# Attention and two gated layers: the maxima of k and q are bound behind the last VectorE operation of the iteration before

## The chip, the core and the metric

The program runs on one NeuronCore of a Trainium2 chip. The core has five engines with a queue of their own each: TensorE (PE in the profile, with PEld for its weight loads), VectorE (DVE), ScalarE (ACT), GpSimd (POOL) and SyncE (SP), which here only starts transfers between DRAM and the on-chip memory. Each queue is worked off in order; engines wait for one another through semaphores. The metric is the time of one execution on the device in microseconds (us), lower is better.

## What is computed

```python
# q, k, v: 8 batches, 8 heads, 576 tokens, 64 features, float32
q_s = exp(q - max(q, features)) ; q_s /= sum(q_s, features) + 1e-9
k_s = exp(k - max(k, tokens))   ; k_s /= sum(k_s, tokens) + 1e-9
attn = q_s @ (k_s^T @ v)                       # per batch and head
x = attn as 4608 tokens x 512 features
xn = x / sqrt(mean(x*x) + 1e-6) * rms_g
x = (silu(xn @ w_gate) * (xn @ w_val)) @ w_out # 512 -> 1536 -> 512
h = max(x @ w1, x @ w2, x @ w3)                # 512 -> 768
out = h @ w_out2                               # 768 -> 512
```

## The kernel before

The 4608 tokens are nine groups of 512: groups 0 to 7 are the first 512 tokens of one batch each, group 8 the last 64 tokens of all eight. Heads go in four pairs (128 features) per group. float32 products are made of three products of parts: an operand is split into a high part (`hh`, `xh`, `qh`, `kvh`) by ScalarE and the remainder (`hl`, `xl`, `ql`, `kvl`) by VectorE.

The first layer runs as 9 x 12 iterations: group g, block f of 128 of the 1536 hidden features. An iteration makes twelve gate products into the PSUM bank `pg` (L691), and twelve value products into `pv` (L703); ScalarE applies tanh (L697), VectorE multiplies it with the gate bank (L698), which empties that bank, then with the value bank (L709); ScalarE rounds the result to `hh` (L712), VectorE takes the remainder `hl` (L716). That is the last VectorE operation of the iteration proper. The output products of block f - 1 follow on PE (L720). There is one gate bank, so the next iteration's gate products need L698 done.

While group g goes through the first layer, the attention of group g + 1 (`nxt`) is prepared pair by pair: at f = 2p the maxima of k and q of pair p (L665, L666: `k_max` at L346, `q_exp` at L324); at f = 2p + 1 k's exponential and q's sum; at f = 2p + 2 q and k^T v are completed and the next pair is loaded; at f = 2p + 3 the attention product follows. For groups 2 to 8 (`by_feature`) q lies in memory twice, by token and by feature. The copy by token gives the statistics: VectorE's maximum (L326), POOL's subtraction (L336), ScalarE's exponential (L337), VectorE's sum (L304) and reciprocal (L307). Maximum and reciprocal are stored to a small DRAM array (L293) and read back spread over partitions (L299); with them POOL subtracts and multiplies on the copy by feature (L310, L315). Groups 0 and 1 (`COMPACT`) go another way. Beside this, group 0's iterations unpack the first layer's weights on VectorE and ScalarE, and groups 1 to 7 split the second layer's weights on ScalarE and POOL and store them to DRAM.

The code's order is not the queues' order. A scheduler places each engine's instructions when the program is built, by their dependencies and its own idea of durations; an instruction whose inputs and buffers it thinks ready may be placed long before the code around it. `k` and `q` tiles have two buffers, the transposed k for the maximum has one.

Of the kernel before, what the change touches and what calls it, by code (L numbers as in the profile page):

```python
# [8 lines left out]
F32 = mybir.dt.float32  # L9
# [38 lines left out]
def attention_moe_moe(ctx: ExitStack, tc: tile.TileContext, q, qt, k, kt, v, w1, rms_g, w2, w2_out, out):  # L48
# [14 lines left out]
    nc = tc.nc  # L63
# [52 lines left out]
    for i in range(2):  # L116
        t = one.tile([P, P], F32, tag=f"kv_raw{i}", name=f"kv_raw{i}")
# [168 lines left out]
    def load_by_feature(g, p):  # L286
        qT[g, p] = two.tile([P, N], F32, tag="qT", name=f"qT_{g}_{p}", bufs=1)
        nc.sync.dma_start(qT[g, p], qt[g - BY_FEATURE, p])

    def put_stat(g, p, i, stat):  # L290

        dst = stats_dram[NPAIR * g + p][i].rearrange("a (r t) -> r a t", t=4)
        nc.sync.dma_start(dst, stat.rearrange("r (a t) -> r a t", a=2))  # L293
# [30 lines left out]
    def q_exp(g, p):  # L324
        qm = two.tile([P, 24], F32, tag="qm", name=f"qm_{g}_{p}")[:, 0:8]
        nc.vector.tensor_reduce(qm, q_t[g, p], axis=AX.X, op=ALU.max)  # L326
        if g in COMPACT:
            qs = two.tile([P, 8], F32, tag="qs", name=f"qs_{g}_{p}")
            qsum[g, p] = qs
            nc.vector.tensor_scalar(qm, qm, -1.0, None, op0=ALU.mult)  # L330
            for i in range(8):
                head = q_t[g, p][:, i, :]
                nc.scalar.activation(head, head, AF.Exp, bias=qm[:, i : i + 1], accum_out=qs[:, i : i + 1])
            return
        put_stat(g, p, 0, qm)
        nc.gpsimd.tensor_sub(q_t[g, p], q_t[g, p], qm.unsqueeze(2).to_broadcast([P, 8, 64]))  # L336
        nc.scalar.activation(q_t[g, p], q_t[g, p], AF.Exp)  # L337
# [8 lines left out]
    def k_max(g, p):  # L346
        if g == NB:
            return
        km = two.tile([P, 1], F32, tag="km", name=f"km_{g}_{p}")
        nc.vector.tensor_reduce(km, kT_t[g, p], axis=AX.X, op=ALU.max)  # L350
        kmax[g, p] = km
# [11 lines left out]
    def make_kv(g, p):  # L363
        if g == NB:
            return
        pk = pair_bank(g, p, "pk", "a0")
        for c in range(5):
            nc.tensor.matmul(  # L368
                pk[:, 0 : P + 1], k_t[g, p][:, c, :], v_t[g, p][:, c, :], start=(c == 0), stop=(c == 4)
            )  # L370
        sm = two.tile([P, 1], F32, tag="ks", name=f"ks_{g}_{p}")
        nc.vector.tensor_scalar(sm, pk[:, P : P + 1], EPS_SM, None, op0=ALU.add)
        rs = two.tile([P, 1], F32, tag="kr", name=f"kr_{g}_{p}")
        nc.vector.reciprocal(rs, sm)
        raw = kv_raw[p % 2]
        for j in range(2):
            s = slice(64 * j, 64 * j + 64)
            nc.vector.tensor_scalar(raw[s, s], pk[s, s], rs[s, 0:1], None, op0=ALU.mult)
        if g not in WHOLE:
            kvh[g, p] = two.tile([P, P], F32R, tag="kvh", name=f"kvh_{g}_{p}")  # L380
            kvl[g, p] = two.tile([P, P], F32R, tag="kvl", name=f"kvl_{g}_{p}")
            split(kvh[g, p], kvl[g, p], raw)
        nc.sync.dma_start(kv_dram[p, :, g, :], raw)
# [122 lines left out]
    def normalise(g, p):  # L506
        if g == 0:
            nc.vector.tensor_mul(xraw[g, p], xraw[g, p], rstd[g][1])
            return
        nc.vector.scalar_tensor_tensor(  # L510
            xraw[g, p], xraw[g, p], gain[:, p : p + 1], rstd[g][1], op0=ALU.mult, op1=ALU.mult
        )
# [45 lines left out]
        for h in range(2):  # L558
            stage(0, h)

    acc, hh, hl = {}, {}, {}

    def out1(g, f):
        if f == 0:
# [82 lines left out]
    def iteration(g, nxt, f):  # L647
        ahead = g == 0 and f + 1 < NF1
        pair, odd = f // 2, f % 2

        if ahead:
            first.scale(f + 1, 0)
        if nxt is not None:
            by_feature = nxt >= BY_FEATURE
            if not odd and 1 <= pair <= 4:
                (q_by_feature if by_feature else transpose_q)(nxt, pair - 1)
                make_kv(nxt, pair - 1)
                if pair + 1 < 4:
                    load_pair(nxt, pair + 1)
            if not odd and pair < 4 and by_feature:  # L660
                load_by_feature(nxt, pair)
            if odd and 1 <= pair <= 4:
                make_x(nxt, pair - 1)
            if pair < 4 and not odd:
                k_max(nxt, pair)  # L665
                q_exp(nxt, pair)  # L666
            if pair < 4 and odd:
                k_exp(nxt, pair)
                (q_stats if by_feature else q_divide)(nxt, pair)
            if f == 10 and nxt in COMPACT:  # L670
                token_rstd(nxt)
            elif f == 10:
                variance(nxt)
                newton_step(nxt, 0)
                newton_step(nxt, 1)
            if f == 11:
                if nxt not in COMPACT:
                    newton_step(nxt, 2)
                for p in range(4):
                    normalise(nxt, p)  # L680
        elif f == 1:
            load_raw(0)
        if ahead:
            first.join(f + 1, 0)
            first.scale(f + 1, 1)
        wkey = (1, f)
        raw = g == 0 and f < NRAW
        xhs = [(rawh[p] if raw else xh[g, p]) for p in range(4)]
        xls = [(rawl[p] if raw else xl[g, p]) for p in range(4)]
        pg = bank("G", f"pg_{g}_{f}")  # L690
        product_in(pg, wh[wkey], wl[wkey], 0, xhs, xls)  # L691
        t = two.tile([P, N], F32, tag="t", name=f"t_{g}_{f}", bufs=1)
        if raw:
            u = two.tile([P, N], F32, tag="y", name=f"u_{g}_{f}", bufs=3)
            nc.vector.tensor_mul(u, pg, rstd[0][1])
            pg = u
        nc.scalar.activation(t, pg, AF.Tanh, scale=0.5)  # L697
        nc.vector.scalar_tensor_tensor(t, t, 1.0, pg, op0=ALU.add, op1=ALU.mult)  # L698
        if ahead:
            first.high(f + 1, 0)  # L700
            first.join(f + 1, 1)
        pv = bank("V", f"pv_{g}_{f}")
        product_in(pv, wh[wkey], wl[wkey], 1, xhs, xls)  # L703
        if nxt is not None and f == 11:
            for p in range(4):
                split_x(nxt, p)
        if raw:
            nc.vector.tensor_mul(t, t, rstd[0][1])
        nc.vector.tensor_mul(t, t, pv)  # L709
        hh[g, f] = two.tile([P, N], F32R, tag="hh", name=f"hh_{g}_{f}")  # L710
        hl[g, f] = two.tile([P, N], F32R, tag="hl", name=f"hl_{g}_{f}")
        nc.scalar.copy(hh[g, f], t)  # L712
        if ahead:
            first.low(f + 1, 0)
            first.high(f + 1, 1)
        nc.vector.tensor_sub(hl[g, f], t, hh[g, f].bitcast(F32))  # L716
        if nxt is not None and f == 9 and nxt not in COMPACT:
            split_squares(nxt)
        if f > 0:
            out1(g, f - 1)  # L720
        elif g > 0:
            out1(g - 1, NF1 - 1)
        if nxt in COMPACT and f == 10:
            spread_rstd(nxt)
        if g > 0 and nxt is not None:
            if g == 1 and f == 0:
                second.load()
                second.load()
            second.advance(f)
            if g == NG - 2 and f == NF1 - 1:  # L730
                assert not second.steps
        if nxt is None:
            if 1 <= f <= 3:
                fetch(2)
            if f in (4, 5):
                for n in range(4 * f - 16, 4 * f - 12):
                    combine(0, n)
            if f >= 6:
                for which in {6: (B11,), 7: (T2,), 8: (T1,), 9: (T3,), 10: (B21, B22), 11: (T4,)}[f]:
                    split_operand(which)  # L740
        if ahead:
            first.low(f + 1, 1)
            first.load(f + 4)
        if g == 0 and f == NRAW - 1:
            for p in range(4):
                normalise(0, p)
                split_x(0, p)

    for g in range(NG):
        nxt = g + 1 if g + 1 < NG else None  # L750
# [177 lines left out]
    for pr in range(NPAIR):  # L928
        behind = []
        for u in range(UNITS):  # L930
            fp, j = divmod(u, 3)
            if j == 0:
                t = {
                    key: two.tile([P, N], F32, tag=tag, name=f"t2_{pr}_{fp}_{tag}")
                    for key, tag in (((0, 0), "q"), ((0, 1), "k"), ((1, 0), "v"))
                }
# [22 lines left out]
    g = NG - 1  # L959
# [28 lines left out]
    for u in range(UNITS):  # L988
        fp, j = divmod(u, 3)
        pair = [bank(tag, f"p2_{g}_{u}_{tag}") for tag in (("G", "V"), ("a0", "a1"))[u % 2]]  # L990
        if j == 0:
            t = [two.tile([P, N], F32, tag=tag, name=f"t2_{g}_{fp}_{tag}") for tag in ("q", "k")]
# [82 lines left out]
```

## Time and profile before

| | |
|---|---|
| median of 3 runs | 1574.95 us (1574.34 to 1579.06) |
| profiled execution | 1573.16 us |
| its span, first to last instruction | 1571.4 us |
| busy share of the span: TensorE, VectorE, ScalarE, GpSimd | 97%, 60%, 37%, 17% |
| groups 1 and 2, from the first gate product of one group to the next | 127.4 and 123.9 us |
| groups 3 to 6 | 106.3 or 106.4 us each |

The profile is of one execution. Times within it count from the first instruction. A matmul's shown duration overlaps the next one's, so a busy TensorE need not be at its peak. Names are those of the program without buffer numbers; L698 is line 698.

### The profile page before, as it was taken

What the parts mean: (1) busy time and instruction counts of PE and PEld (TensorE: products, weight loads), DVE (VectorE), ACT (ScalarE), POOL (GpSimd) and SP (SyncE); (2) the same over time, 40 slices, a digit from 0 to 9 for tenths busy, and PEclk for the clock granted to TensorE, in tenths of its full rate; (3) what the DMA queues carried; (4) which work ended last, traced back from release to release, by engine and by line L of the source; (5) the groups of instructions that cost most, each with busy time, mean ns of one, the idle gap of its engine ahead of it and who ended that gap; (6) DMA issues with size and microseconds to landing.
All of it is one profiled execution on the core that took longest, in us unless ns stands there. A gap on an engine that the chain in (4) does not pass through costs nothing.

```text
span 1571.4 us, 19245 instructions
## 1 busy us (share of the span) xinstructions
PE 1517.6 (97%) x6790; PEld 1244.1 (79%) x6790; DVE 938.2 (60%) x1622; ACT 579.0 (37%) x1107; POOL 263.7 (17%) x307
## 2 busy tenths in 40 slices
PE   6899988889999999999999999999999999999999
PEld 4677876767888888888888888888888888888887
DVE  6999765754655546555444252527947937937722
ACT  6764434433433433334333231322412412413311
POOL 0000234233131131231321100001111111111100
PEclk8899999999999999999999999999999999999999
DMA  7842655564343442552433204026576486485573
GB/s 272 321 154 76 197 134 148 129 122 131 117 143 93 156 154 63 173 166 75 144 118 121 74 7 168 1 87 242 173 273 239 158 295 234 159 306 198 164 271 107
DMA packets 126065, 250.03 MB, mean 159 GB/s; under 512 B 26640, under 2 KB 51216, under 8 KB 125968
## 3 DMA queue, kind: packets, MB, share of 16 engines
q1 hardware_dynamic: 119056, 236.21, 46.3%
q10 hardware_dynamic: 6912, 12.59, 2.4%
q8 instruction: 54, 0.88, 0.2%
q14 instruction: 43, 0.35, 0.1%
HBM read 205.52 MB, written 43.22 MB: 158 GB/s over the span
## 4 chain that ended last, share of the span: by engine, by line
PE 75%; DVE 1%; POOL 0%; DMA 0%; issue 0%; ACT 0%; SPq 0%; ACTq 0%; DVEq 0%
PE pg L523 5%; PE acc L530 5%; PE acc L531 5%; PE acc L529 4%; PE pg L525 4%; PE pg L524 4%; PE pv L525 4%; PE pv L524 4%; PE pv L523 4%; PE p_a L530 4%; PE p_a L531 4%; PE p_a L529 4%; PE p_G L529 2%; PE p_G L530 2%; PE p_G L531 2%; PE p_V L531 1%
## 5 line engine op out<-in xcount | busy, mean ns | idle before, releaser
L698 DVE SCALAR_TENSOR_TENSOR t<-t,pg 128x512 f32<-128x512 f32 x106 | 72.6, 685 | 117.0 <-ACT t L697 115.4
L800 POOL TENSOR_TENSOR temps_wl<-temps_wh 128x512 f32<-128x512 f32 x36 | 48.3, 1341 | 438.3 <-ACT temps_wh L799 363.7
L712 ACT CAST hh<-t 128x512 fp32r<-128x512 f32 x108 | 66.8, 619 | 126.4 <-DVE t L709 125.9
L709 DVE TENSOR_TENSOR t<-t,pv 128x512 f32<-128x512 f32 x108 | 73.9, 684 | 65.2 <-PE pv L525 63.2
L716 DVE TENSOR_TENSOR hl<-t,hh 128x512 fp32r<-128x512 f32 x108 | 76.0, 704 | 52.6 <-ACT hh L712 52.3
L697 ACT ACTIVATE t<-pg 128x512 f32<-128x512 f32 x106 | 62.9, 593 | 87.9 <-PE pg L525 87.7
L529 PE MATMUL p_a<-x_wh,chunk 128*128 128x512 f32 x240 | 93.4, 389 | 0.0
L531 PE MATMUL p_a<-x_wh,chunk 128*128 128x512 f32 x240 | 93.4, 389 | 0.0
L530 PE MATMUL p_a<-x_wl,chunk 128*128 128x512 f32 x236 | 91.8, 389 | 0.0
L236 POOL TENSOR_TENSOR wq<-st,wq 128x256 fp32r<-128x256 f32 x84 | 63.6, 773 | 110.0 <-ACT wq L235 87.6
L795 ACT COPY temps_wh<-p_G 128x512 f32<-128x512 f32 x36 | 21.1, 587 | 104.4 <-PE p_G L531 104.2
L427 POOL TENSOR_TENSOR sacc<-sacc,sq 128x512 f32<-128x512 f32 x21 | 27.2, 1293 | 182.2 <-ACT sq L426 172.2
L315 POOL TENSOR_TENSOR qT<-qT,stat 128x512 f32<-128x512 f32 x28 | 37.6, 1344 | 92.9 <-DMA stat<-stats 70.3
L529 PEld LDWEIGHTS p_a<-x_wh,chunk 128*128 128x128 f32 x240 | 45.0, 188 | 9.4
L531 PEld LDWEIGHTS p_a<-x_wh,chunk 128*128 128x128 f32 x240 | 45.0, 188 | 9.3
L336 POOL TENSOR_TENSOR q<-q,qm 128x512 f32<-128x512 f32 x28 | 33.9, 1220 | 106.9 <-DVE qm L326 67.4
L310 POOL TENSOR_TENSOR qT<-qT,stat 128x512 f32<-128x512 f32 x28 | 37.3, 1333 | 85.2 <-DMA stat<-stats 85.2
L530 PEld LDWEIGHTS p_a<-x_wl,chunk 128*128 128x128 f32 x236 | 44.3, 188 | 9.2
L529 PE MATMUL p_G<-x_wh,chunk 128*128 128x512 f32 x123 | 48.2, 392 | 0.2
L531 PE MATMUL p_G<-x_wh,chunk 128*128 128x512 f32 x123 | 47.9, 389 | 0.0
L93 DVE TENSOR_TENSOR ql<-qT,qh 128x512 fp32r<-128x512 f32 x24 | 17.1, 712 | 47.5 <-ACT qh L92 47.5
L368 PEld LDWEIGHTS pk<-v,k 128*128 128x128 f32 x300 | 38.4, 195 | 8.7 <-issue 4.4
(689 smaller groups left out, 4508.5 us busy)
## 6 DMA issues: line engine op xcount, KB each, us to landing
chunk<-w_dram SPq DMA_DIRECT2D x112, 768.0 KB, 4.4
w_dram<-wq SPq DMA_DIRECT2D x84, 256.0 KB, 2.7
words<-in_w SPq DMA_DIRECT2D x24, 768.0 KB, 8.3
stat<-stats SPq DMA_DIRECT2D x112, 128.0 KB, 3.2
chunk<-w_dram SPq DMA_DIRECT2D x48, 256.0 KB, 3.6
k<-in_k SPq DMA_DIRECT2D x30, 320.0 KB, 4.1
v<-in_v SPq DMA_DIRECT2D x30, 320.0 KB, 4.7
st<-in_w SPq DMA_DIRECT2D x18, 512.0 KB, 4.9
```

The source lines that it names most:

```text
L236: nc.gpsimd.tensor_sub(t[:, 1, :], src, t[:, 0, :].bitcast(F32))
L523: nc.tensor.matmul(pt, hi[:, j, s], xhs[kk], start=(kk == 0), stop=False)
L524: nc.tensor.matmul(pt, hi[:, j, s], xls[kk], start=False, stop=False)
L525: nc.tensor.matmul(pt, lo[:, j, s], xhs[kk], start=False, stop=(kk == 3))
L529: nc.tensor.matmul(pt, ah, bh, start=first, stop=False, skip_group_check=onto)
L530: nc.tensor.matmul(pt, ah, bl, start=False, stop=False, skip_group_check=onto)
L531: nc.tensor.matmul(pt, al, bh, start=False, stop=last, skip_group_check=onto)
L697: nc.scalar.activation(t, pg, AF.Tanh, scale=0.5)
L698: nc.vector.scalar_tensor_tensor(t, t, 1.0, pg, op0=ALU.add, op1=ALU.mult)
L709: nc.vector.tensor_mul(t, t, pv)
L712: nc.scalar.copy(hh[g, f], t)
L716: nc.vector.tensor_sub(hl[g, f], t, hh[g, f].bitcast(F32))
```

## The change

The remainder instructions (`hl`) are kept in a list. For groups prepared by feature, the maxima are traced inside `tc.issue_after(x)`, which adds an ordering edge from each instruction in the block that runs on x's engine to x. x is the last `hl` made, that of the iteration before, so on VectorE the two maxima (L350 and L326) may not be placed ahead of it. The block's instructions on other engines get no edge.

```diff
--- before.py
+++ after.py
@@ -558,7 +558,7 @@
         for h in range(2):
             stage(0, h)
 
-    acc, hh, hl = {}, {}, {}
+    acc, hh, hl, lows = {}, {}, {}, []
 
     def out1(g, f):
         if f == 0:
@@ -662,8 +662,9 @@
             if odd and 1 <= pair <= 4:
                 make_x(nxt, pair - 1)
             if pair < 4 and not odd:
-                k_max(nxt, pair)
-                q_exp(nxt, pair)
+                with tc.issue_after(lows[-1].ins) if by_feature else ExitStack():
+                    k_max(nxt, pair)
+                    q_exp(nxt, pair)
             if pair < 4 and odd:
                 k_exp(nxt, pair)
                 (q_stats if by_feature else q_divide)(nxt, pair)
@@ -713,7 +714,7 @@
         if ahead:
             first.low(f + 1, 0)
             first.high(f + 1, 1)
-        nc.vector.tensor_sub(hl[g, f], t, hh[g, f].bitcast(F32))
+        lows.append(nc.vector.tensor_sub(hl[g, f], t, hh[g, f].bitcast(F32)))
         if nxt is not None and f == 9 and nxt not in COMPACT:
             split_squares(nxt)
         if f > 0:
```

In the new file lines behind the edit are numbered higher, by one where the rows below show it (L698 becomes L699). VectorE's queue in group 1, iterations 4 and 5; in the names the first number is the group, the second the iteration (`hl`, `t`) or the pair (`qm`, `qs`, `km`). Before:

```order
L716 TENSOR_TENSOR hl_1_4_1939<-t_1_4_1921,hh_1_4_1938 128x512
L304 TENSOR_REDUCE qs_3_2_2937<-q_3_2_2676 128x8
L326 TENSOR_REDUCE qm_3_3_3037<-q_3_3_2847 128x8
L358 TENSOR_TENSOR k_2_2_1712<-k_2_2_1712,pb_2_2_1977 128x640
L350 TENSOR_REDUCE km_3_0_2509<-kT_3_0_2487 128x1
L305 TENSOR_SCALAR qs_3_2_2937<-qs_3_2_2937 128x8
L304 TENSOR_REDUCE qs_3_3_3105<-q_3_3_2847 128x8
L307 RECIPROCAL qr_3_2_2940<-qs_3_2_2937 128x8
L305 TENSOR_SCALAR qs_3_3_3105<-qs_3_3_3105 128x8
L307 RECIPROCAL qr_3_3_3108<-qs_3_3_3105 128x8
L698 SCALAR_TENSOR_TENSOR t_1_5_2005<-t_1_5_2005,pg_1_5_1992 128x512
L709 TENSOR_TENSOR t_1_5_2005<-t_1_5_2005,pv_1_5_2008 128x512
```

The same place after the change:

```order
L717 TENSOR_TENSOR hl_1_4_1939<-t_1_4_1921,hh_1_4_1938 128x512
L358 TENSOR_TENSOR k_2_2_1712<-k_2_2_1712,pb_2_2_1977 128x640
L699 SCALAR_TENSOR_TENSOR t_1_5_2005<-t_1_5_2005,pg_1_5_1992 128x512
L710 TENSOR_TENSOR t_1_5_2005<-t_1_5_2005,pv_1_5_2008 128x512
L93 TENSOR_TENSOR ql_2_2_2047<-qT_2_2_1899,qh_2_2_2046 128x512
L717 TENSOR_TENSOR hl_1_5_2023<-t_1_5_2005,hh_1_5_2022 128x512
L350 TENSOR_REDUCE km_2_3_2069<-kT_2_3_1889 128x1
L326 TENSOR_REDUCE qm_2_3_2071<-q_2_3_1891 128x8
```

The maxima and sums of group 3's q and k have left group 1's iterations; those of group 2's own pair 3 stand behind `hl` of iteration 5. In the whole of VectorE's queue, 18 maxima of q stood between the last `hl` of group 0 and that of group 1, and 9 in the next group; now 4 stand in each group.

VectorE's queue at the start of group 4. Before:

```order
L716 TENSOR_TENSOR hl_3_11_4386<-t_3_11_4352,hh_3_11_4385 128x512
L698 SCALAR_TENSOR_TENSOR t_4_0_4443<-t_4_0_4443,pg_4_0_4430 128x512
L709 TENSOR_TENSOR t_4_0_4443<-t_4_0_4443,pv_4_0_4446 128x512
L716 TENSOR_TENSOR hl_4_0_4461<-t_4_0_4443,hh_4_0_4460 128x512
L358 TENSOR_TENSOR k_5_0_4405<-k_5_0_4405,pb_5_0_4496 128x640
L350 TENSOR_REDUCE km_5_2_4785<-kT_5_2_4600 128x1
```

After the change:

```order
L717 TENSOR_TENSOR hl_3_11_4386<-t_3_11_4352,hh_3_11_4385 128x512
L350 TENSOR_REDUCE km_5_0_4423<-kT_5_0_4401 128x1
L326 TENSOR_REDUCE qm_5_0_4425<-q_5_0_4403 128x8
L304 TENSOR_REDUCE qs_5_0_4500<-q_5_0_4403 128x8
L305 TENSOR_SCALAR qs_5_0_4500<-qs_5_0_4500 128x8
L307 RECIPROCAL qr_5_0_4503<-qs_5_0_4500 128x8
L699 SCALAR_TENSOR_TENSOR t_4_0_4443<-t_4_0_4443,pg_4_0_4430 128x512
L710 TENSOR_TENSOR t_4_0_4443<-t_4_0_4443,pv_4_0_4446 128x512
L717 TENSOR_TENSOR hl_4_0_4461<-t_4_0_4443,hh_4_0_4460 128x512
```

Group 5's first pair has both maxima, q's sum and its reciprocal between the last `hl` of group 3 and the first operation on group 4's gate bank. On ScalarE the exponential of that q now stands between the last `hh` of group 3 and the tanh of group 4.

## Rows read from the trace of the kernel before

**Rows 1.** The page: span; busy time, share, instructions; granted clock in 40 slices.
```profile
span 1571.4 us, 19245 instructions
...
PE 1517.6 (97%) x6790; PEld 1244.1 (79%) x6790; DVE 938.2 (60%) x1622; ACT 579.0 (37%) x1107; POOL 263.7 (17%) x307
...
PEclk8899999999999999999999999999999999999999
```

**Rows 2.** Stretches, groups 0 to 3: length, busy us (instructions) per engine, clock, DMA.
```profile
52.00:161.10 109.10, 106.36 (x476) 84.11 (x477) 107.16 (x181) 66.13 (x136) 3.75 (x10) 0.98 0.48 159
161.10:288.50 127.40, 114.03 (x491) 90.93 (x489) 87.83 (x175) 50.26 (x94) 46.38 (x50) 0.96 0.56 147
288.50:412.40 123.90, 112.64 (x490) 90.09 (x491) 73.00 (x148) 47.55 (x88) 35.36 (x40) 0.97 0.50 123
412.40:518.70 106.30, 106.30 (x491) 88.41 (x490) 57.98 (x105) 40.93 (x76) 23.78 (x30) 1.00 0.40 125
```

**Rows 3.** Lines L326 and L336: count, ns min/median/max, first and last start.
```profile
L326 DVE TENSOR_REDUCE qm<-q x34: 660/682/690, 4.5 to 348.7; 128x8 f32<-128x512 f32 x34
...
L336 POOL TENSOR_TENSOR q<-q,qm x28: 1036/1136/1603, 146.0 to 349.5; 128x512 f32<-128x512 f32 x28
```

**Rows 4.** Waits of PE's weight loads, 161 to 412.4 us: total, times, longest.
```profile
PEld pg L523 <- DVE t L698: 13.4, 11, 3.4
```

**Rows 5.** VectorE in group 1 by time: start, length, line, op [idle before <- releaser].
```profile
270.85 0.69 DVE L304 TENSOR_REDUCE qs<-q 128x8 f32<-128x512 f32 x1 [1.60 <-ACT q L337]
272.99 0.69 DVE L326 TENSOR_REDUCE qm<-q 128x8 f32<-128x512 f32 x1 [1.45 <-DMA q<-in_q]
273.59 0.16 DVE L305 TENSOR_SCALAR qs<-qs 128x8 f32<-128x8 f32 x1
...
274.00 0.20 DVE L307 RECIPROCAL qr<-qs 128x8 f32<-128x8 f32 x1
...
275.67 0.69 DVE L304 TENSOR_REDUCE qs<-q 128x8 f32<-128x512 f32 x1
...
276.88 0.68 DVE L698 SCALAR_TENSOR_TENSOR t<-t,pg 128x512 f32<-128x512 f32 x1
```

**Rows 6.** PE by time, at the end of that stretch.
```profile
277.61 0.63 PE L523 MATMUL pg<-xh,wh_(1, 11)_1407 128*128 128x512 f32 x1 [2.98 <-DVE t L698]
```

**Rows 7.** Instruction groups: shapes, count | busy us, mean ns | idle before, releasers.
```profile
L336 POOL TENSOR_TENSOR q<-q,qm 128x512 f32<-128x512 f32 x28 | 33.9, 1220 | 106.9 <-DVE qm L326 67.4 <-DVE a L472 21.9 <-ACT hh L712 5.6
...
L326 DVE TENSOR_REDUCE qm<-q 128x8 f32<-128x512 f32 x34 | 23.0, 680 | 18.6 <-DMA q<-in_q 16.9 <-DMA stats<-qm 1.6
...
L350 DVE TENSOR_REDUCE km<-kT 128x1 f32<-128x576 f32 x29 | 21.6, 745 | 4.3 <-DMA kT<-in_kt 4.3
...
L304 DVE TENSOR_REDUCE qs<-q 128x8 f32<-128x512 f32 x28 | 18.8, 679 | 11.6 <-ACT q L337 11.4
...
L337 ACT ACTIVATE q<-q 128x512 f32<-128x512 f32 x28 | 17.6, 631 | 41.1 <-POOL q L336 40.8 <-POOL v L272 0.4
```

**Rows 8.** VectorE by time, start of group 4 (iterations 0 to 2).
```profile
520.23 0.69 DVE L716 TENSOR_TENSOR hl<-t,hh 128x512 fp32r<-128x512 f32 x1 [0.69 <-ACT hh L712]
522.28 0.69 DVE L698 SCALAR_TENSOR_TENSOR t<-t,pg 128x512 f32<-128x512 f32 x1 [1.36 <-ACT t L697]
...
534.06 0.69 DVE L716 TENSOR_TENSOR hl<-t,hh 128x512 fp32r<-128x512 f32 x1 [0.69 <-ACT hh L712]
...
541.15 0.69 DVE L698 SCALAR_TENSOR_TENSOR t<-t,pg 128x512 f32<-128x512 f32 x1
```

**Rows 9.** PE by time: first gate products of iterations 1 and 3 there.
```profile
526.92 0.47 PE L523 MATMUL pg<-xh,wh_(1, 1)_526 128*128 128x512 f32 x1
...
545.25 0.48 PE L523 MATMUL pg<-xh,wh_(1, 3)_724 128*128 128x512 f32 x1
```

**Rows 10.** DMA issues: count, KB each, median us from issue to landing.
```profile
stat<-stats SPq DMA_DIRECT2D x112, 128.0 KB, 3.2
...
stats<-qr SPq DMA_DIRECT2D x28, 4.0 KB, 4.5
```

## The prediction

> **What bounds the kernel now.** The page comes first: PE (TensorE) is busy 97% of a span of 1571.4 us, at the full clock almost everywhere [rows 1]. That reads like a kernel with nothing left. The table by stretch says otherwise. Groups 3 to 6 issue the same 490 or so matmuls each as groups 1 and 2, and take 106.3 or 106.4 us with PE never idle; group 3 stands for the four. Group 1 takes 127.4 us, group 2 takes 123.9 us [rows 2]. So 21.1 + 17.6 = 38.7 us lie in two groups whose PE work is no larger. What differs is the other engines: VectorE is busy 87.8 and 73.0 us there against 58.0, POOL (GpSimd) 46.4 and 35.4 against 23.8.
>
> What fills them is seen by asking when line L326 (the maxima of q) and line L336 (subtracting them) run. All 28 subtractions, four for each of groups 2 to 8, start between 146.0 and 349.5 us [rows 3], though group 8's q is wanted only while group 7 is computed. The scheduler lets the softmax of q run up to five groups early, and groups 1 and 2 pay. How they pay is in the waits of PE's weight loads in that stretch: longest in total is the first gate product waiting for VectorE's L698, which empties the gate bank [rows 4]. One case: L698 starts at 276.88, behind a q sum that had waited 1.60 us for ScalarE, a q maximum that had waited 1.45 us for its q to arrive, and a second sum [rows 5]; PE's next product starts at 277.61, after 2.98 us of idleness [rows 6]. A queue runs in order: a piece of work that nobody needs yet, waiting for its own input, holds up one that PE needs now.
>
> [...]
>
> **The change, part by part.** No instruction is added or removed. For groups 2 to 8 the maxima of k and q of pair p are held, on VectorE alone, behind the last VectorE operation of the iteration before (hl). What hangs on them moves along: two statistic stores and the q loads on SP's queue, POOL's subtraction, ScalarE's exponential, VectorE's sum and reciprocal.
>
> *Groups 1 and 2.* 27 of the 28 maxima of q stand there now; afterwards 4 do in each. Their excess over group 3 is what I expect to go: -38.7 us. Bounds: all of it, or, if the staging of the second weights (which starts in group 1) were to blame for some, the 24.6 us of plain PE idleness. I take all, because groups 3 to 7 stage weights at the same pace and PE does not idle there.
>
> *Group 0.* VectorE is busy 107.2 of 109.1 us: it is the bound there [rows 2]. Two early instructions leave it, a k maximum of 0.745 us and a q maximum of 0.680 us [rows 7]: -1.4 at most, 0 at least if something else closes the gap. I take -1.3.
>
> *Groups 3 to 7* receive four q chains each. Per pair that is 0.68 + 0.68 + 0.36 us on VectorE [rows 5, 7], 1.22 on POOL, 0.63 on ScalarE [rows 7]: 6.9 us on VectorE's 58 of 106.3. Load is no problem; position is. Two places matter.
>
> First the start of a group. Before, L698 of iteration 0 runs at 522.28, 1.36 us after hl ends at 520.92 [rows 8]. Now maxima, sum and reciprocal stand between them in VectorE's queue, and the exponential stands ahead of tanh on ScalarE. From 520.92: + 0.745 + 0.68 = 522.35, POOL's subtraction + 1.22 = 523.57, exponential + 0.63 = 524.20, sum + 0.68 = 524.88, the two small ones 0.16 + 0.20 [rows 5], L698 + 0.69: it ends at 525.93. PE wants the gate bank again at 526.92 [rows 9]. The cover is 0.99 us, less whatever three handovers between engines cost. At worst I lose half a microsecond at each of 7 group starts, at best nothing; I take +1.0. The same delay moves the evacuation of the value bank, which has a further 12 products of slack.
>
> Second, pairs 1 to 3. hl of iteration 1 ends at 534.75 [rows 8]; the same sum puts the q sum's end at 534.75 + 0.745 + 0.68 + 1.22 + 0.63 + 0.68 = 538.71. L698 runs at 541.15 now, held by other work, and PE wants the bank at 545.25 [rows 8, 9]: 3.4 us of cover. A subtraction that queues on POOL behind twice its own length (2 x 1.22) would still leave 1.0. Bounds 0 and 0.5 us for each of 21 pairs; I take +1.5.
>
> *The statistics' way through DRAM* becomes part of the chain. After the reciprocal, near 525.3, come a store (4.5 us) and a spread back (3.2 us) [rows 10], at 533.0; then multiply, round and subtract, which I bound by the three steps of rows 7 (1.22 + 0.63 + 0.68): 535.5. PE needs the result in iteration 3, just ahead of 545.25 [rows 9]: some 9 us of cover. For later pairs the two buffers that hold spread statistics are free only when PE has used up the previous pair's q, as before. Cost: nothing, hidden by two iterations of matmuls; uncovered it would be 0 to 8 us a pair.
>
> *SP's queue.* A statistic store now sits among weight stores and k, v loads, and whatever follows waits until the reciprocal is there. The k load for the next pair now waits for a maximum that comes up to three iterations later than before; its own maximum is due two iterations after that. I cost this at nothing, covered by the same slack.
>
> **Sum.** -38.7 - 1.3 + 1.0 + 1.5 = -37.5 us. The profiled execution took 1573.16 us (span 1571.4), 1.8 under the median of 1574.95. 1573.16 - 37.5 = 1535.7; I forecast 1536.
>
> **Rivals.**
>
> *The waits come back, smaller, in all seven groups.* VectorE now stands still in each pair between maximum and sum, waiting for POOL and ScalarE. For it: at a group start the cover is under 1 us. Against it: elsewhere it is 3.4 us. If each of 28 pairs cost PE 0.3 to 0.8 us, 8 to 22 us come back in place of my 2.5: 1541 to 1556.
>
> *PE's low clock stays.* Groups 1 and 2 show a granted clock of 0.96 and 0.97, groups 3 to 7 show 1.00 [rows 2]; 0.04 x 127.4 + 0.03 x 123.9 = 8.8 us of the excess is clock. If these stretches at 1.2 GHz came for a reason other than the idle gaps, they stay: 1535.7 + 8.8 = 1544.5. The Trainium skill (TensorE: Matmul & The Clock Gate, What's actually happening) says the reverse, that activity lifts the throttle and idleness brings it back; by that rule the 8.8 us go with the gaps, and groups 3 to 7 agree, busy throughout at 1.00.
>
> *Nothing changes.* The excess would come from something else that starts in group 1. Against it: rows 5 name q's own waits. Time 1573 to 1575.
>
> *Slower.* The place is the gate bank, the mechanism that VectorE's stand of 1.22 + 0.63 us plus handovers, about 2.05 us a pair, has no cover. It decides from the point where L698 ends later than PE's next gate product wants the bank: 0.99 us later than my sum at a group start, 3.4 us at the other pairs. Then all 28 pay: 28 x 2.05 = 57 us against 40.0 gained, 1573.2 - 40.0 + 57.4 = 1590.6. Covers of 3.4 us at 21 of 28 places speak against it.
>
> **How the numbers follow.** Forecast 0.75, with its own range 1531 to 1541; small waits everywhere 0.13; clock stays 0.04; nothing 0.04; slower 0.04. The low end is the whole excess and group 0 gone without any loss, 1573.2 - 40.1 = 1533, less 3 for the run; the high end takes most of the small-waits rival in: 1530 to 1552. About 0.3% (4.7 us) is what a measurement here can tell from no change. Faster by more than that: 0.75 + 0.13 + 0.04 = 0.92; within it 0.04; slower 0.04.
>
> **What would show it.** In the profile after, L326 and L336 spread from about 165 to 850 us, four to a group; groups 1 and 2 within 2 us of 106.3, granted clock 1.00; no PE wait for L698 over 1 us outside group starts. Should group 3 grow past 109 us, the first rival holds; should groups 1 and 2 keep more than 115 us with the maxima gone from them, I misread the cause.

## The result, and the profile after

The changed kernel takes 1540.68 us, median of 5 runs (1538.83 to 1543.83), against 1574.95 us (5 runs, 1573.24 to 1579.06): 0.9777 of the time before, with an interval of 0.9756 to 0.9798. The forecast was 1536 us with a range of 1530 to 1552. The profiled execution took 1538.84 us, 34.3 less than the 1573.16 before, where the sum had 37.5.

The page after; the rows answer to [rows 1].

```profile
span 1537.0 us, 19169 instructions
...
PE 1503.1 (98%) x6790; PEld 1238.1 (81%) x6790; DVE 939.8 (61%) x1622; ACT 578.4 (38%) x1107; POOL 259.1 (17%) x307
...
PEclk9999999999999999999999999999999999999999
```

The busy shares barely differ from before. By the shares alone one would not see that 2% of the time is gone.

The table by stretch of the kernel after, groups 0 to 4; here group 0 counts from its own first gate product, so its row is longer than the first of [rows 2].

```profile
37.40:157.90 120.50, 112.16 (x508) 89.04 (x507) 117.45 (x213) 74.63 (x159) 0.82 (x8) 0.97 0.53 185
157.90:270.60 112.70, 108.48 (x492) 88.01 (x491) 67.26 (x128) 44.73 (x84) 28.73 (x36) 1.00 0.43 128
270.60:377.40 106.80, 106.56 (x492) 88.49 (x491) 63.11 (x118) 42.83 (x79) 28.23 (x34) 1.00 0.46 130
377.40:483.70 106.30, 106.30 (x491) 88.40 (x490) 64.84 (x121) 43.35 (x80) 28.20 (x34) 1.00 0.46 136
483.70:590.00 106.30, 106.30 (x491) 88.42 (x490) 64.32 (x121) 44.44 (x83) 29.67 (x37) 1.00 0.47 143
```

Group 1 went from 127.4 to 112.7 us, group 2 from 123.9 to 106.8, and the clock in both from 0.96 and 0.97 to 1.00. VectorE's and GpSimd's work now lies evenly: 58.0 us of VectorE in group 3 became 64.8, 87.8 in group 1 became 67.3. The account, from first gate product to first gate product:

| stretch | before | after | difference |
|---|---|---|---|
| up to group 0's first gate product | 37.6 | 37.4 | -0.2 |
| group 0 | 123.5 | 120.5 | -3.0 |
| group 1 | 127.4 | 112.7 | -14.7 |
| group 2 | 123.9 | 106.8 | -17.1 |
| groups 3 to 7 together | 531.0 | 531.5 | +0.5 |
| the rest | 628.0 | 628.1 | +0.1 |
| span | 1571.4 | 1537.0 | -34.4 |

When the maxima of q (L326) and their subtraction (L336) run, after: count, least/median/greatest ns, first and last start. They answer to [rows 3].

```profile
L326 DVE TENSOR_REDUCE qm<-q x34: 664/675/686, 4.7 to 859.4; 128x8 f32<-128x512 f32 x34
...
L336 POOL TENSOR_TENSOR q<-q,qm x28: 1042/1045/1418, 163.1 to 860.2; 128x512 f32<-128x512 f32 x28
```

The 28 subtractions that all started before 349.5 us reach to 860.2 us, four in each of groups 1 to 7.

What PE's weight loads wait for after the change, first in group 1 (157.9 to 270.6 us), all three lines that there are; they answer to [rows 4]:

```profile
PEld pg L523 <- DVE t L699: 3.5, 4, 1.1
PEld px L408 <- ACT kvh L92: 2.9, 2, 1.8
PEld px L410 <- DVE kvl L93: 1.1, 4, 0.4
```

In groups 2 to 7 together (270.6 to 908.9 us) this is the only line:

```profile
PEld pg L523 <- DVE t L699: 1.0, 2, 0.6
```

Before, the gate bank was the largest of PE's waits in groups 1 and 2 but not the only one: of 24.6 us of idleness there it was 10.0, and the rest were waits for `kvh` (4.0), `hl` (3.0) and others.

```profile
PE pg L523 <- DVE t L698: 10.0, 10, 3.0
```

So what is left is in group 1, which keeps 6.4 us over 106.3, and half of its waits are of a kind not named ahead: the attention product (`px`, L408 to L410) waits for the parts of k^T v. It does so twice. First the three engines behind the earlier wait, by time. VectorE:

```profile
180.27 0.69 DVE L93 TENSOR_TENSOR ql<-qT,qh 128x512 fp32r<-128x512 f32 x1 [2.63 <-ACT qh L92]
...
180.94 0.68 DVE L326 TENSOR_REDUCE qm<-q 128x8 f32<-128x512 f32 x1
...
181.72 0.58 DVE L378 TENSOR_SCALAR kv_raw<-pk,kr 64x64 f32<-64x64 f32 x2
184.29 0.69 DVE L304 TENSOR_REDUCE qs<-q 128x8 f32<-128x512 f32 x1 [1.99 <-ACT q L337]
```

GpSimd:

```profile
178.28 1.30 POOL L315 TENSOR_TENSOR qT<-qT,stat 128x512 f32<-128x512 f32 x1 [1.86 <-DMA stat<-stats]
180.69 0.88 POOL L236 TENSOR_TENSOR wq<-st,wq 128x256 fp32r<-128x256 f32 x1 [1.11 <-ACT wq L235]
...
181.85 0.75 POOL L236 TENSOR_TENSOR wq<-st,wq 128x256 fp32r<-128x256 f32 x1
182.55 1.04 POOL L336 TENSOR_TENSOR q<-q,qm 128x512 f32<-128x512 f32 x1
```

ScalarE:

```profile
179.61 0.62 ACT L92 CAST qh<-qT 128x512 fp32r<-128x512 f32 x1 [3.55 <-DMA w_dram<-wq]
...
183.63 0.63 ACT L337 ACTIVATE q<-q 128x512 f32<-128x512 f32 x1 [2.00 <-POOL q L336]
184.17 0.28 ACT L92 CAST kvh<-kv_raw 128x128 fp32r<-128x128 f32 x1
```

And PE:

```profile
183.44 0.39 PE L531 MATMUL acc<-hh,wl_(1, 1)_549 128*128 128x512 f32 x1
184.50 0.50 PE L408 MATMUL px<-qh,kvh 128*128 128x512 f32 x1 [0.68 <-ACT kvh L92]
```

Read from the end: PE waits for `kvh`. Its input `kv_raw` was there at 182.30, but `kvh` stands on ScalarE behind the exponential of the next pair's q, which waited 2.00 us for GpSimd's subtraction. That started at 182.55, behind pieces of the second layer's weights (L236), though the maximum it needs was there at 181.62. A bound q chain and the staging of weights meet here, and each stands in a queue in front of something that PE wants.

The later wait is the longest that PE has in group 1, 1.41 us, and it goes through VectorE:

```profile
198.86 0.69 DVE L93 TENSOR_TENSOR ql<-qT,qh 128x512 fp32r<-128x512 f32 x1 [2.68 <-ACT qh L92]
...
200.74 0.68 DVE L326 TENSOR_REDUCE qm<-q 128x8 f32<-128x512 f32 x1
...
201.85 1.34 DVE L215 SCALAR_TENSOR_TENSOR st<-st 128x512 int32<-128x512 int32 x1
...
203.91 0.67 DVE L304 TENSOR_REDUCE qs<-q 128x8 f32<-128x512 f32 x1
204.50 0.57 DVE L378 TENSOR_SCALAR kv_raw<-pk,kr 64x64 f32<-64x64 f32 x2
```

```profile
205.46 0.50 PE L408 MATMUL px<-qh,kvh 128*128 128x512 f32 x1 [1.41 <-ACT kvh L92]
```

The last k^T v product had ended at 195.8, but `kv_raw` comes at 204.50: `ql` held VectorE's queue for 2.68 us until `qh` was there, and the next pair's maximum, pieces of the staging (L214 to L216) and q's sum followed ahead of it. So the staging has a part on VectorE too (L214 to L216, L228 to L231), beside those on ScalarE and GpSimd.

Why group 1 and not the later groups, which stage as much? Its first chain starts late. VectorE is busy 117.5 of group 0's 120.5 us, and its last `hl` ends 3.8 us after group 1's first gate product, where in groups 2 to 6 it ends 0.1 us after. Then pieces of staging stand between q's sum and its reciprocal:

```profile
160.97 0.68 DVE L717 TENSOR_TENSOR hl<-t,hh 128x512 fp32r<-128x512 f32 x1
...
168.51 0.20 DVE L307 RECIPROCAL qr<-qs 128x8 f32<-128x8 f32 x1
```

From the end of `hl` to the end of the reciprocal that is 7.1 us, against 4.2 at the start of group 4. `qh` starts 21.8 us into group 1 and 14.3 to 16.2 us into groups 2 to 6, `kvh` 26.3 against 21.0 to 22.0 us; in groups 2 to 6 the attention product stands at 25.8 us.

### The profile page after: what moved, and what is told of

Read it like the earlier page. It is cut to its first block, busy times and chain, and to the rows that moved or that the text cites. A ratio compares the mean times of both kernels' runs of the same rounds, so it can differ in the third digit from the quotient of the medians.

```text
span 1537.0 us, 19169 instructions
## 1 busy us (share of the span) xinstructions
PE 1503.1 (98%) x6790; PEld 1238.1 (81%) x6790; DVE 939.8 (61%) x1622; ACT 578.4 (38%) x1107; POOL 259.1 (17%) x307
## 4 chain that ended last, share of the span: by engine, by line
PE 84%; DVE 8%; DMA 3%; issue 2%; POOL 1%; ACT 1%; SPq 0%; POOLq 0%; ACTq 0%; DVEq 0%
PE pg L523 6%; PE pg L525 5%; PE pg L524 5%; PE acc L529 5%; PE acc L530 5%; PE acc L531 5%; PE pv L523 5%; PE pv L524 5%; PE pv L525 5%; PE p_a L531 4%; PE p_a L530 4%; PE p_a L529 4%; PE p_G L529 2%; PE p_G L531 2%; PE p_G L530 2%; PE pk L368 2%
## 5 line engine op out<-in xcount | busy, mean ns | idle before, releaser
L699 DVE SCALAR_TENSOR_TENSOR t<-t,pg 128x512 f32<-128x512 f32 x106 | 72.3, 682 | 112.2 <-ACT t L698 110.3
L698 ACT ACTIVATE t<-pg 128x512 f32<-128x512 f32 x106 | 62.7, 591 | 88.6 <-PE pg L525 87.2
L236 POOL TENSOR_TENSOR wq<-st,wq 128x256 fp32r<-128x256 f32 x84 | 64.2, 779 | 39.0 <-ACT wq L235 34.3
L336 POOL TENSOR_TENSOR q<-q,qm 128x512 f32<-128x512 f32 x28 | 30.3, 1083 | 209.7 <-DVE qm L326 178.5
L796 ACT COPY temps_wh<-p_G 128x512 f32<-128x512 f32 x36 | 21.1, 586 | 104.5 <-PE p_G L531 104.2
L310 POOL TENSOR_TENSOR qT<-qT,stat 128x512 f32<-128x512 f32 x28 | 37.5, 1340 | 132.3 <-DMA stat<-stats 132.3
L337 ACT ACTIVATE q<-q 128x512 f32<-128x512 f32 x28 | 17.7, 632 | 75.1 <-POOL q L336 67.4
L798 DVE TENSOR_TENSOR temps_wh<-temps_wh,p_V 128x512 f32<-128x512 f32 x36 | 24.6, 683 | 33.4 <-PE p_V L531 33.4
```

The source lines that it names most:

```text
L236: nc.gpsimd.tensor_sub(t[:, 1, :], src, t[:, 0, :].bitcast(F32))
```

## The experiments

Each row gives the ratio to the kernel before on the same chip. "Excess" is a group's length over 106.3 us, and the counts are the subtractions L336 that start in groups 0, 1 and 2; 28 in all, of which four belong in each of groups 1 to 7.

| kernel | median us | ratio and interval | counts | excess of groups 1, 2 |
|---|---|---|---|---|
| before | | | 1, 17, 10 | 21.1, 17.6 |
| the change | 1540.68 | 0.9777 (0.9756 to 0.9798) | 0, 4, 4 | 6.4, 0.5 |
| only q's maxima bound | 1547.56 | 0.9792 (0.9774 to 0.9810) | 0, 4, 4 | 5.9, 1.6 |
| only k's maxima bound | 1571.32 | 0.9938 (0.9916 to 0.9960) | 1, 18, 9 | 22.6, 12.3 |
| bound from group 5 on | 1553.70 | 0.9828 (0.9802 to 0.9855) | 1, 11, 0 | 17.3, 0.0 |
| lead of up to 13 iterations | 1541.64 | 0.9756 (0.9737 to 0.9775) | 1, 7, 4 | 4.9, 0.0 |
| GpSimd's step three times | 1574.91 | 0.9964 (0.9948 to 0.9980) | | 13.4, 6.4 |
| group 2's maxima free | 1539.64 | 0.9746 (0.9730 to 0.9762) | 1, 3, 4 | 0.0, 1.0 |
| weights staged from group 2 | 1541.91 | 0.9767 (0.9747 to 0.9788) | 0, 4, 4 | 1.3, 1.0 |
| lead 4 | 1538.19 | 0.9738 (0.9722 to 0.9754) | 0, 5, 4 | 5.1, 2.1 |
| lead 4 and staging from 2 | 1539.34 | 0.9763 (0.9748 to 0.9777) | 0, 5, 4 | 1.7, 2.4 |
| lead 2 and staging from 2 | 1533.43 | 0.9722 (0.9707 to 0.9737) | 0, 5, 3 | 0.0, 0.0 |
| lead 2 | 1536.02 | 0.9728 (0.9712 to 0.9743) | 0, 5, 4 | 2.5, 0.0 |
| the change, run again | 1539.25 | 0.9760 (0.9740 to 0.9781) | 0, 4, 4 | 5.8, 0.0 |

"Lead n" means that the maxima are bound behind the n-th last `hl`, so lead 1 is the change itself.

**Which of the two maxima matters.** Only q's is bound:

```diff
             if pair < 4 and not odd:
+                k_max(nxt, pair)
                 with tc.issue_after(lows[-1].ins) if by_feature else ExitStack():
-                    k_max(nxt, pair)
                     q_exp(nxt, pair)
```

> Only q's maxima are bound behind the preceding hl; k's maxima are free again. Theory A (q's softmax running up to five groups early crowds groups 1 and 2): q is all that ran far ahead, k has one buffer for its maximum and could not; the whole gain stays, 1537 to 1543 us, and group 2 takes under 108 us. Theory B (what matters is that no maximum, k's or q's, stands in front of the gate bank's operation inside an iteration): the k maxima come back in front of it and take part of the gain, 1548 to 1560 us.

And only k's:

```diff
                 with tc.issue_after(lows[-1].ins) if by_feature else ExitStack():
                     k_max(nxt, pair)
-                    q_exp(nxt, pair)
+                q_exp(nxt, pair)
```

> Only k's maxima are bound; q's are free. In VectorE's queue q runs up to 62 iterations early again. Theory A: nothing of the gain is left, 1570 to 1577 us, groups 1 and 2 take 120 us or more each. Theory B: half of it is left, 1548 to 1560 us.

Binding q alone gives 0.9792, whose interval overlaps that of the whole change; in the traces its groups 1 to 7 are together still 4.4 us longer than the change's (755.5 against 751.1), so k's part is small but perhaps not nothing. Binding k alone leaves the q chains crowded in groups 1 and 2 and the time at 0.9938. The stretches of groups 1 and 2 with only k bound:

```profile
163.20:292.20 129.00, 115.11 (x492) 90.57 (x491) 88.97 (x177) 51.76 (x96) 46.25 (x51) 0.96 0.60 142
292.20:410.70 118.50, 111.06 (x490) 88.89 (x491) 70.13 (x144) 46.52 (x86) 36.83 (x40) 0.99 0.50 128
```

VectorE and GpSimd are as full in group 1 as in [rows 2], and the clock is low again with them. Group 2 is 5.4 us shorter than before; this small gain was not foreseen, and no run here explains it.

**How much the crowding costs.** The binding begins with group 5, so the chains of groups 2 to 4 stay early:

```diff
-                with tc.issue_after(lows[-1].ins) if by_feature else ExitStack():
+                with tc.issue_after(lows[-1].ins) if nxt >= 5 else ExitStack():
```

> The maxima of groups 5 to 8 are bound, those of groups 2 to 4 are free. Groups 3 and 4 have their eight q pairs computed early, in group 1 and at the start of group 2, in place of 24 pairs in the kernel before. Theory A, with a price per pair computed early of 38.7 us / 24 = 1.6 us: 8 x 1.6 = 13 us over an undisturbed 1534, 1544 to 1551 us, the excess all in group 1 and the first iterations of group 2. If running early is harmless until the queues are full: 1534 to 1540. If any lead at all is what costs: 1560 or more.

Its groups 1 and 2:

```profile
161.20:284.80 123.60, 113.99 (x492) 91.42 (x491) 80.52 (x158) 48.84 (x92) 38.08 (x44) 0.96 0.53 141
284.80:391.10 106.30, 106.30 (x491) 88.41 (x490) 55.95 (x102) 40.52 (x75) 23.50 (x30) 1.00 0.38 120
```

Eleven chains fall into group 1, seven too many, and cost 17.3 us there, 2.5 a piece. Group 2 has none and loses nothing. Before, 13 too many in group 1 cost 21.1 us (1.6 each) and 6 too many in group 2 cost 17.6 (2.9 each): there is no one price per chain.

**Whether being early is the harm, or being many.** Here the chains may run a whole group early, but no further:

```diff
-                with tc.issue_after(lows[-1].ins) if by_feature else ExitStack():
+                with tc.issue_after(lows[-13].ins) if by_feature and len(lows) >= 13 else ExitStack():
```

> The maxima are bound behind the hl made 13 iterations of list earlier in place of 1: q may run 12 iterations, one whole group, early, and does from group 3 on. Theory A: only the four pairs that build up the lead in group 1 cost something, 4 x 1.6 = 6.5 us there; after that each group computes four pairs as in the bound kernel, so 1537 to 1545 us. If standing close to its use is what makes the bound kernel fast: each group pays, 1550 us or more.

0.9756, as good as the change. By the counts all four chains of group 3 run in group 1, and so on to group 8's in group 6: 24 of 28 run in the group before the usual one (and group 2's first in group 0, as before the change). Groups 2 to 7 are all at 106.3 us or below. Being early costs nothing. What costs is that many chains share one group's iterations. How is shown in [rows 5]: each can stand in VectorE's queue ahead of something that PE wants, the gate bank most often, while it waits for another engine.

**How much cover the pairs have.** On GpSimd q has its maximum subtracted, added and subtracted again, so the chain is longer by two of its steps:

```diff
-        nc.gpsimd.tensor_sub(q_t[g, p], q_t[g, p], qm.unsqueeze(2).to_broadcast([P, 8, 64]))
+        spread = qm.unsqueeze(2).to_broadcast([P, 8, 64])
+        nc.gpsimd.tensor_sub(q_t[g, p], q_t[g, p], spread)
+        nc.gpsimd.tensor_add(q_t[g, p], q_t[g, p], spread)
+        nc.gpsimd.tensor_sub(q_t[g, p], q_t[g, p], spread)
```

> The bound kernel with q's maximum subtracted, added and subtracted again on POOL: two further 128x512 operations of about 1.08 us each between the maximum and the exponential of every pair, 2.2 us on VectorE's stand. It prices the covers of the prediction. With 0.99 us of cover at 7 group starts and 3.4 us at the other 21 pairs: 7 x (2.2 - 0.99) = 8 us over the bound kernel, ratio about 0.983, the loss at the first gate product of iteration 1 of each group. With no cover (the rival that ended slower): 28 x 2.2 = 62 us, ratio about 1.017. With more cover than reckoned: ratio 0.978.

The span is 1578.5 us, 41.5 more than the change's; by the ratios it is about 30 (0.0187 x 1580), and the profiled execution was the slowest of ten (1580.28 us, median 1574.91). Every group from 2 to 7 is longer than in the change, by 4.3 to 5.9 us, and group 1 by 7.0. Group 3 of this kernel, and what PE's weight loads wait for in groups 3 to 7 of it (391.9 to 949.2 us; L702 is the operation on the gate bank, three lines further down than in the change):

```profile
391.90:504.10 112.20, 109.41 (x492) 89.40 (x491) 68.00 (x121) 43.35 (x80) 37.55 (x42) 0.98 0.46 129
```

```profile
PEld pg L526 <- DVE t L702: 17.1, 11, 3.1
```

Two more steps of about 1.04 us are 2.1 us a pair, which a cover of 3.4 us would have swallowed. It did not, and the ratio is 0.9964 where about 0.983 was expected: in groups 2 to 6 the operation on the gate bank ends too late at iterations 2 and 4. So at most of these places the cover was under 2.1 us, as the trace of the change has it (0.5 to 3.3 us, below). Of the group starts this run says nothing: the scheduler placed q's sum behind the operation on the gate bank there (in group 4 the maximum at 504.80, the operation at 507.64, the sum at 509.54). And 0.02 of 112.2 us, 2.2 us a group, is the low clock that came back with the waits.

**What group 1 keeps.** Two theories for the remaining 6.4 us were that the binding of group 2's own maxima does it, which have to be ready in group 1, or that the staging of the second layer's weights does it, which begins in group 1. The first, with group 2's maxima left free:

```diff
-                with tc.issue_after(lows[-1].ins) if by_feature else ExitStack():
+                with tc.issue_after(lows[-1].ins) if nxt > BY_FEATURE else ExitStack():
```

> As the bound kernel, but group 2's four maxima are free and run 1 to 3 iterations early; groups 3 to 8 are bound. It asks what is left over in group 1 (112.7 us against 106.3). Theory C (group 2's first statistics come too late, its remainder ql holds VectorE's queue with the next maximum behind it): group 1 falls to 106 to 108 us; group 0, bound by VectorE, takes back its two maxima, +1 to +3 us; ratio 0.973 to 0.976. Theory D (the staging of the second weights that starts in group 1): group 1 stays at 111 to 113, ratio 0.978 to 0.980.

The second, with the staging begun a group later:

```diff
-            room = 3 if 1 <= f <= 8 else 2
+            room = 3 if f <= 9 else 2
...
-        if g > 0 and nxt is not None:
-            if g == 1 and f == 0:
+        if g > 1 and nxt is not None:
+            if g == 2 and f == 0:
                 second.load()
```

> The bound kernel, with the staging of the second layer's weights begun in group 2 in place of group 1 and with a little more of it per group (iterations 0 and 9 take one more unit of it). Theory D: group 1 has nothing beside its four pairs and falls to 106.3 us; 6 us less than the bound kernel, ratio 0.974. Theory C: group 1 stays at 110 us or more, ratio 0.977 to 0.979.

Group 1 with group 2's maxima free, then with the later staging:

```profile
160.90:267.20 106.30, 106.30 (x491) 88.40 (x490) 67.07 (x125) 43.96 (x82) 27.03 (x34) 1.00 0.43 130
```

```profile
159.10:266.80 107.70, 107.26 (x492) 88.33 (x492) 60.52 (x115) 38.98 (x69) 18.91 (x23) 1.00 0.32 88
```

Either is enough to take most of it away, so it needs both, as the rows at 180 to 205 us show: a bound chain that comes late meets staging on the queues of VectorE, GpSimd and ScalarE. Neither kernel is clearly faster than the change. With group 2 free, group 0 takes 2.8 us more again (123.3 us); with the later staging, groups 3 and 5 take 109.6 and 108.4 us. In that group 3 the first `hl` is late as well: it starts 1.9 us after the group's first gate product, and 0.6 us before it in groups 2, 4, 5 and 6.

**A middle lead.** The maxima may run up to four iterations early, or two, with and without the later staging. The edit for two:

```diff
-                with tc.issue_after(lows[-1].ins) if by_feature else ExitStack():
+                with tc.issue_after(lows[-2].ins) if by_feature and len(lows) >= 2 else ExitStack():
```

> The maxima are bound behind the hl made four iterations earlier, so q runs up to 3 iterations early (1 for group 2's first two pairs). Theory A with theory C: the statistics have three iterations more of cover, group 1 at 107 to 109 us, later groups at 106.3, ratio 0.974 to 0.976. Theory A with theory D: group 1 at 111 to 112, later groups at 106.3, ratio 0.976 to 0.978.

> Both remedies together: q up to three iterations early, and the staging of the second weights from group 2. If group 1's remainder needs the staging and late statistics at once, and the small waits of groups 2 to 6 need a lead of zero, then groups 1 to 6 all stand at 106.3 us, group 0 at 121, and the span is 121 + 6 x 106.3 + 105.7 + 628 + 37.6 = 1530 us, ratio 0.969 to 0.973. If the lead only moves the wait to group starts (in the kernel with lead 4 alone group 2 took 108.4 us), 0.973 to 0.976, no better than lead 4 alone.

> As before with q one iteration early. The first maximum of a group then stands before the x remainders of the group start, so the start is as in the kernel before, and the statistics have one iteration more. Same forecast as for lead 4, 0.969 to 0.974; should a lead of one be too short for the statistics, small waits of 0.5 to 2 us come back in groups 2 to 6 and it lies between the bound kernel with late staging (0.9767) and lead 4.

> A lead of one iteration alone, with the second weights staged from group 1 as in the bound kernel. It asks which half of the last kernel (ratio 0.9722, groups 1 to 7 at 105.9 to 106.3 us) did it. If the lead removes the small waits of groups 2 to 6 and the staging is what was left in group 1: group 1 at 110 us or more, all others at 106.3, ratio 0.974 to 0.977. If one iteration of lead cures group 1 as well: all at 106.3, 0.971 to 0.973.

> The bound kernel once more, beside the others on one chip: ratio 0.976 to 0.980, group 1 at 111 to 114 us, the other groups between 106.3 and 108, with the small waits in other places than in its first profile if they come from transfers' arrival, and in the same places if they come from the order of the queues.

With lead 4 groups 1 and 2 keep 7.2 us (111.4 and 108.4 us long, so the 107 to 109 us expected of group 1 failed, though the ratio of 0.9738 is as low as forecast for that case), with a wait of a kind of its own at a group's start, where the first gate product waits for the high part of x; the later staging takes 3.4 us from group 1 but the ratio is no better (0.9763), so the hoped-for 0.969 to 0.973 failed. From the weight-load waits with lead 4:

```profile
PEld pg L523 <- ACT xh L92: 2.0, 1, 2.0
```

Lead 2 does best. With the later staging its page and its groups 1 and 2 read

```profile
span 1531.4 us, 19162 instructions
```

```profile
159.60:265.90 106.30, 106.30 (x491) 88.41 (x490) 62.04 (x116) 39.50 (x69) 21.64 (x24) 1.00 0.34 89
265.90:372.30 106.40, 106.40 (x492) 88.45 (x492) 61.42 (x116) 43.17 (x82) 28.51 (x36) 1.00 0.45 140
```

and from 159.6 to 904 us PE's weight loads have one line of waits:

```profile
PEld pg L523 <- DVE t L699: 0.3, 1, 0.3
```

At 1533.43 us (1531.72 to 1533.82) it beats the kernel before (0.9722) and, by its interval, the change as first timed. Timed side by side on one chip, lead 2 alone and the change took 1536.02 (1534.05 to 1536.81) and 1539.25 us (1538.81 to 1545.19); the medians differ by 3.2 us, the intervals of the ratios just touch, and in the traces group 1 alone differs by 3.3 us (108.8 against 112.1). The first `kvh` of group 1 starts 26.3 us into the group in the change (184.17), 22.5 us with lead 2 and 21.0 us with the later staging too: the next pair's exponential no longer stands ahead of it. Group 1 with lead 2 alone:

```profile
159.80:268.60 108.80, 107.20 (x492) 88.33 (x490) 70.07 (x129) 45.29 (x85) 32.62 (x37) 1.00 0.45 133
```

Most of its remaining 2.5 us is one stop of PE, 1.51 us at 196.55 us in front of a k^T v product, for which the profile shows no releaser. Whether the later staging adds to lead 2 is shown by group 1 (106.3 against 108.8) but not settled by the times: 0.9722 and 0.9728 have nearly the same interval.

## Why the prediction was right, and where its terms were not

**The cause held.** It was the maxima of q: binding q alone gives nearly the whole gain, binding k alone about a quarter of it (0.9938). "A piece of work that nobody needs yet holds up one that PE needs now" is right, with one word to add: it takes many of them. A chain a whole group early is harmless (lead 13).

**Groups 1 and 2: -38.7 forecast, -31.8 measured.** This is the term that was too large. Group 2 came to 106.8 us, inside the 2 us that were named; group 1 kept 6.4 us and did not, though it stayed below the 115 us that would have meant a wrong cause. Two steps failed there: "the statistics' way through DRAM" at no cost, and the reason for taking the whole excess, that groups 3 to 7 stage weights at the same pace and PE does not idle. Both hold from group 2 on. In group 1 the chain starts 3.7 us later than in the groups behind it and takes 2.9 us more to its reciprocal: GpSimd's L315 got its spread statistics at 178.28, `qh` came at 179.61, and the next pair's chain and the staging then stood ahead of `kvh` and `kv_raw`. The sum had counted the steps of one pair from an undisturbed group's start, and not what the next pair's chain does to the queues that both go through. The lower bound of 24.6 us, matmul idleness alone (groups 1 and 2 of [rows 2] less PE's 114.0 and 112.6 us), was passed by 7.2 us, so weighing the stretch table over PE's busy time was right. SP's queue was put at nothing; from group 2 on PE's weight loads wait for the gate bank alone, and in group 1 its share was not taken apart.

**Group 0: -1.3 forecast, -3.2 measured** with the stretch ahead of it. Two early instructions left VectorE, a maximum of k at 130.32 and one of q at 145.08 us, and two waits of PE soon behind, for VectorE's L709 and `hl`, went with them. Before:

```profile
151.37 0.50 PE L523 MATMUL pv<-xh,wh_(1, 11)_1407 128*128 128x512 f32 x1 [0.63 <-DVE t L709]
...
154.09 0.50 PE L530 MATMUL acc<-hl,wh_(1, 10)_1326 128*128 128x512 f32 x1 [0.88 <-DVE hl L716]
```

After, PE has no gap between 140 and 157.9 us. These two are 1.5 of the 3.2 us; the rest was not traced to single waits. The term counted the two maxima's own lengths, and the measured gain is more than twice that; what they delayed is a likely reason, not one that a run shows.

**Group starts: +1.0 forecast, none found.** The sum from the end of `hl` to the end of the operation on the gate bank was 5.01 us; at the start of group 4 VectorE shows, after the change:

```profile
483.13 0.69 DVE L717 TENSOR_TENSOR hl<-t,hh 128x512 fp32r<-128x512 f32 x1
483.74 0.75 DVE L350 TENSOR_REDUCE km<-kT 128x1 f32<-128x576 f32 x1
484.40 0.68 DVE L326 TENSOR_REDUCE qm<-q 128x8 f32<-128x512 f32 x1
486.90 0.69 DVE L304 TENSOR_REDUCE qs<-q 128x8 f32<-128x512 f32 x1 [1.82 <-ACT q L337]
...
487.95 0.64 DVE L699 SCALAR_TENSOR_TENSOR t<-t,pg 128x512 f32<-128x512 f32 x1
```

It ends at 488.59, 4.77 us after `hl` at 483.82. The chain was sized well. But `hl` ends 0.12 us after the group's first gate product at 483.70, and before it ended 2.22 us after (520.92 against 518.70): there, a `ql` that had waited 1.84 us for `qh` stood in VectorE's queue ahead of it at 515.25 us, and now none does. PE wants the bank at 491.89, so the cover is 3.3 us and not 0.99.

**Other pairs: +1.5 forecast, +0.5 in groups 3 to 7.** The cover of 3.4 us was read at one iteration and is not a constant. After the change the operation on the gate bank ends 1.6 to 3.3 us early at iteration 2, 0.5 to 3.1 at iteration 4 and 0.1 to 1.5 at iteration 6 (groups 2 to 6). The cost came out small because the chain mostly fits even there: the only waits are 0.24 us in group 2 and 0.23 us in group 5. GpSimd's step made longer by 2.1 us shows how near the edge it is.

**The signs and the rivals.** Two of the signs came: four subtractions in each of groups 1 to 7 at a clock of 1.00, and no stop of PE for the gate bank over 1 us (0.82 at most; its weight loads waited up to 1.1). The third came half: group 2 within 2 us of 106.3, group 1 not. Small waits in all seven groups: no; 0.5 us in groups 3 to 7 together. Nothing changes: no. Slower: no, the gate bank had its cover; GpSimd's step thrice shows what that rival looks like, ratio 0.9964 against 0.9777. The low clock stays: no. Before, the clock records show PE at half clock (1.2 GHz) for 3.4 to 6.8 us at a time at 253.9, 277.8, 349.5 and 366.6 us; after, at no time between 60 us and the end. It came back where the waits came back: in group 1 of the kernel bound from group 5 on, which is at 0.96 there and at 1.00 in group 2, and once in each group with GpSimd's step thrice. This agrees with the Trainium skill (TensorE: Matmul & The Clock Gate, What's actually happening), which has activity lift the throttle and idleness bring it back. No run changed the clock alone, so how much of the 31.8 us is clock is known only by estimate: 8.8 in the forecast, and 8.5 by the clock records, half of the 17.1 us that the four stretches last.

The sum of what was measured: -31.8 - 3.2 + 0.6 = -34.4 us of span, against -37.5. The errors of the terms were +6.9, -1.9 and -1.9 us, and partly cancelled; that the total came within 3.1 us is in part luck.

## What to carry to other kernels

A busy share of 97% says little; compare stretches that do the same products, and ask of the longer ones what else runs in them. When a scheduler lets an off-path chain run early, look at how many share one stretch and at what stands behind each in the queue while it waits for another engine; bounding the lead is enough, and here a lead of one step more than the strictest gave the longest chain slack (group 1: 108.8 against 112.1 us). Cover is a number per place and not per kernel: read it at each iteration where the chain will stand, and read what the next round's chain does to the queues that both share.

## What was not expected

A small stop of PE was followed by the low clock in two kernels and not in others. With lead 4, PE idles 1.58 us in front of the first gate product of group 2 (270.21 us), after a group with 1.8 us of other small stops, and the clock records show it at half clock from 271.3 to 274.7 us; lead 4 with the later staging has the same at the start of group 3 (1.66 us, half clock from 378.4 to 381.8 us). In the change, PE stopped 1.41 us for `kvh` in group 1 and 4.2 us there in all, and the clock stayed at 1.00. No run here tells what makes the difference.

Small waits of 1 to 3 us turn up in different groups from one bound kernel to the next (group 4 with group 2's maxima free, groups 3 and 5 with the later staging), although their chains are bound in the same way there. In the change itself group 1 took 112.7 us in one execution and 112.1 in another, group 2 106.8 and 106.3, group 5 106.9 and 106.3, group 6 106.3 and 107.0, so differences under 1 us in one group say nothing here. The small waits behind group 1 moved although the queues' order is the same; the expectation took that as a sign of transfers that arrive at other times, which no run shows.
